# A linear-attention and gated-FFN kernel: one small transpose moved from TensorE to VectorE, finer weight loads, zero matmuls in later banks, separate places for the last outputs, and a new instruction order

## The chip, the cores and the metric

The kernel runs on one core of a Trainium2 chip. The metric is the device time of one execution in microseconds (us). A kernel is run several times; medians are quoted. Profiles are of one execution each, so a profile's span differs by a fraction of a per cent from the median.

Names used below: TensorE is "PE" in the profile (its weight loads are "PEld"), VectorE is "DVE", ScalarE is "ACT", GpSimd is "POOL" and SyncE is "SP". "SPq", "ACTq" and "POOLq" are DMA issues on an engine's queue. The kernel's matmuls write into eight accumulators of 128 x 512 fp32 in PSUM, called banks here. To "evict" a bank is to copy its result out of PSUM.

## The reference

```python
# q, k, v: [8 batches, 8 heads, 576 rows, 64]; w_phi: [64, 128]
def phi(x):
    proj = x @ w_phi
    proj = proj - max(abs(proj), axis=-1)
    return concat([exp(proj), exp(-proj)], axis=-1)

q_p, k_p = phi(q), phi(k)
kv  = k_p^T @ v                       # per batch and head
num = q_p @ kv
den = q_p . sum(k_p over rows) + 1e-6
x   = (num / den), heads side by side # [4608, 512]
out = (relu(x @ w_gate) * (x @ w_val)) @ w_out   # 512 -> 1536 -> 512
```

The subtraction of the row's maximum does not cancel: it scales the first half of the features by exp(-m) and the second half by exp(+m) after the sign is worked in. The kernel therefore takes plain exponentials and applies, for every row of q, a scale exp(2m). To get it, m has to be brought from "one row of a tile for each maximum" to "one partition for each row of q". This small turn is what the change is about.

## The kernel before

All operations are listed once in a plan, and a fixed table (`ORDER`) says in which order each engine issues them and which ring slot or bank each takes. An entry like `196P0` is operation 196 on TensorE with slot 0; `w21` is 21 zero matmuls that keep TensorE active while it has nothing to do. The kernel before has these at the start only, always in the last bank:

```python
    def warm():
        nc.tensor.matmul(warm_bank[:, 0:P], lhsT=zero, rhs=zero)
...
ORDER = """
0G 3D 9S 4D 1S 8S 11S 10S 5G 7S 6D w21 34P00 15S0 35D w3 32P1 2D 13S w1 56P230000 33A ...
"""      # over a hundred such lines
```

q's scale, done 11 times (7 times for the main rows, 4 times for the rest rows of 64): TensorE turns the maxima (`away`), VectorE reduces over the 4 groups (`amax`) and expands the result (`spread`), and a TensorE matmul in fp32 with a picking matrix brings it back (`back`).

```python
    def q_scale(mq, zq, cq, n, deps, key):
        ps = bank()
        cols = NQ * n
        one, pick = (one_a, pick_a) if n > H else (one_b, pick_b)

        def away():
            nc.tensor.matmul(ps.t[0:cols, 0:P], lhsT=mq.t..., rhs=ident32, is_transpose=True)

        def amax():
            nc.vector.tensor_reduce(ps.t[0:cols, 2 * P : 2 * P + 32], ps.t[0:cols, 0:P]..., op=ALU.max)

        def spread():
            nc.vector.tensor_tensor(zq.t[0:cols], ps.t[0:cols, None, 2 * P : 2 * P + 32]...,
                                    one[0:cols]..., op=ALU.mult)

        def back():
            nc.tensor.matmul(ps.t[:, P : P + n], lhsT=zq.t[0:cols]..., rhs=pick[0:cols])

        def ex():
            nc.scalar.activation(cq.t, ps.t[:, P : P + n], AF.Exp, scale=2.0)
        ...
```

The FFN weights come in three equal pieces of 512 columns, loaded by GpSimd's queue:

```python
    NS = 3
    def load_wide(t, w, i, key, deps=()):
        cols = slice(DFF // NS * i, DFF // NS * (i + 1))
        ...nc.gpsimd.dma_start(out=t[:, :, cols], in_=w.rearrange("(c p) n -> p c n", p=P)[:, :, cols])
```

The end of each FFN group: four blocks of 12 matmuls into a bank, an eviction by ScalarE or VectorE into one of two buffers, and a store. The last group holds the rest rows and stores each block in two parts:

```python
        "ob": ring("ob", 2, [P, DM], FP32),
        ...
        for t in range(4):
            ps, ob = bank(), buf("ob")
            ...                                   # 12 matmuls of 512 columns
            def cp(eng, ps=ps, ob=ob):
                f = nc.scalar.copy if eng is nc.scalar else eng.tensor_copy
                f(ob.t, ps.t)

            def store(t=t, ob=ob):
                if g < B:
                    ... one store on SyncE's queue
                else:
                    for x in range(2):
                        r0 = S * (2 * t + x) + SF
                        nc.sync.dma_start(out=out[r0 : r0 + SM, :], in_=ob.t[SM * x : SM * (x + 1), :])
```

## Time and profile before

| | kernel before |
|---|---|
| median of the first 3 runs | 389.31 us (389.22 to 390.38) |
| median of the 4 runs beside the changed kernel | 389.85 us (389.22 to 390.73) |
| span of the profiled execution | 388.1 us |
| TensorE's last matmul ends at | 382.40 us |
| first FFN matmul / first one of 256 columns | 34.77 / 40.61 us |

The profile page of the kernel before, first its busy time per engine, then TensorE's busy tenths and granted clock in 40 slices of the span, then its three FFN groups ("busy, mean ns of one | idle before, what ended it"):

```profile
PE 371.2 (96%) x3302; PEld 209.6 (54%) x3348; DVE 268.7 (69%) x673; ACT 234.0 (60%) x525; POOL 167.4 (43%) x199
PE   7788999999999999999999999999999999999994
PEclk9998999999999999999999999999999999999999
L714 PE MATMUL ps<-wo_sb,h 128*128 128x512 bf16 x418 | 102.2, 379 | 0.9 <-issue 0.2
L684 PE MATMUL ps<-xT,wg_sb 128*128 128x512 bf16 (+2 forms) x467 | 98.0, 336 | 0.8
L684 PE MATMUL ps<-xT,wv_sb 128*128 128x512 bf16 (+2 forms) x464 | 96.5, 338 | 1.2 <-ACT xT L663 0.2
```

TensorE bounds the kernel, and most of its time is FFN. What is not at its limit is the first four slices (about 39 us) and the last one. The windows view of the kernel before gives the columns: stretch and its length, busy time and count on PE, PEld, DVE, ACT and POOL, granted clock, DMA share, GB/s:

```profile
30.00:35.00 5.00, 3.58 (x54) 2.59 (x53) 4.83 (x16) 4.98 (x11) 3.39 (x5) 0.97 1.22 286
34.00:36.00 2.00, 1.44 (x16) 1.24 (x16) 2.00 (x9) 1.97 (x6) 1.10 (x2) 0.68 0.91 147
36.00:38.00 2.00, 2.00 (x22) 2.00 (x20) 1.78 (x5) 1.79 (x6) 1.37 (x2) 0.50 1.28 206
350.00:370.00 20.00, 19.89 (x93) 9.06 (x93) 5.97 (x10) 4.98 (x9) 0.00 (x0) 1.00 0.07 27
```

Two things are to be seen. From 30 to 35 us TensorE has work for 3.58 of 5 us while VectorE and ScalarE are full; they are the limit there. And from 34.74 to 38.15 us, by the clock record of the trace, TensorE runs at half the clock. In the FFN alone (350 to 370 us), 93 matmuls of 512 columns take 20 us, 215 ns each.

The groups by form of the kernel before that belong to q's scale (7 of its 11 times; the matmul and its weight load appear twice each because an fp32 matmul is issued as two):

```profile
L554 PEld LDWEIGHTS ps<-pick_a,zq 128*128 128x128 f32 x14 | 2.5, 190 | 0.7
L554 PE MATMUL ps<-pick_a,zq 128*128 128x32 f32 x14 | 2.3, 244 | 0.0
L546 DVE TENSOR_TENSOR zq<-ps,one_a 128x128 f32<-128x128 f32 x7 | 2.0, 290 | 0.2
```

One of those fp32 pairs in the timeline of the kernel before, between its neighbours. The pair starts at 63.72 and the next matmuls at 64.04 us: 0.32 us of TensorE for 8 columns.

```profile
63.40 0.40 PE L656 MATMUL ps<-ident,xu 128*128 128x128 bf16 x4
63.72 0.38 PE L554 MATMUL ps<-pick_b,zq 32*128 32x8 f32 x2
64.04 0.42 PE L615 MATMUL ps<-kv,qp 128*128 128x65 bf16 x8
```

The tail of the kernel before, from the timeline. In brackets is the time that an engine was idle, and what it waited for:

```profile
380.73 1.67 PE L714 MATMUL ps<-wo_sb,h 128*128 128x512 bf16 x7
380.93 4.18 SPq L733 DMA_DIRECT2D out_dram<-ob  x5
382.03 0.58 ACT L724 COPY ob<-ps 128x512 f32<-128x512 f32 x1 [3.28 <-DMA out_dram<-ob]
383.39 0.58 ACT L724 COPY ob<-ps 128x512 f32<-128x512 f32 x1 [0.78 <-DMA out_dram<-ob]
```

The last eviction starts at 383.39 us, 1.0 us after the last matmul's end, because it waits for the store that still holds its buffer.

To split the 382.4 us, I costed every TensorE instruction of the order with intervals read from the trace (0.2155 us for 512 columns, 0.109 for 256, 0.055 for 128, 0.031 for 65, and so on) and added them up. This estimate gives about 351 us of work, so about 31.5 us are lost. Comparing the running sum with the clock time at q's first scale transpose (52.59 us, 28.9 us of work done) shows where: 23.7 us before it, about 8 after it.

### The profile page before, as it was taken

Reading aid. Unit: us, or ns where it says so; the run is one execution under the profiler, and the core shown is the slowest. Engines: PE = TensorE matmul, PEld = TensorE weight load, DVE = VectorE, ACT = ScalarE, POOL = GpSimd, SP = SyncE. Lnnn points to the kernel's source line nnn. Section 1 sums busy time; section 2 is a strip of 40 time slices with the busy share of each in tenths; the row PEclk is TensorE's granted clock in tenths of the full one; section 3 lists DMA queues with packets and bytes.
Section 4 is the critical chain, followed back from the end, with each engine's and each line's share of the span. In section 5 each row is a group of like instructions: output and inputs, shape, how many; then the busy total and the mean of one; then the engine's idle time right before and its main releaser. Section 6 shows DMA issues by size and latency. Waiting matters only on the chain.

```text
span 388.1 us, 8687 instructions
## 1 busy us (share of the span) xinstructions
PE 371.2 (96%) x3302; PEld 209.6 (54%) x3348; DVE 268.7 (69%) x673; ACT 234.0 (60%) x525; POOL 167.4 (43%) x199
## 2 busy tenths in 40 slices
PE   7788999999999999999999999999999999999994
PEld 6666798644654455446546454555365444444441
DVE  5899889568787878877876898678867544514130
ACT  3999984389629956694796468953975212212211
POOL 3587935229536932693286246813831300100000
PEclk9998999999999999999999999999999999999999
DMA  7999993879877955685699765277511100200024
GB/s 194 166 136 239 142 173 44 123 146 212 124 118 201 227 130 117 78 114 107 119 207 209 135 98 131 73 171 123 95 57 15 32 10 27 69 27 27 2 108 109
DMA packets 84393, 45.00 MB, mean 116 GB/s; under 512 B 56608, under 2 KB 77728, under 8 KB 84352
## 3 DMA queue, kind: packets, MB, share of 16 engines
q0 software_dynamic: 31744, 21.83, 34.9%
q1 hardware_dynamic: 52528, 22.59, 25.6%
q8 instruction: 26, 0.43, 0.5%
q14 instruction: 15, 0.12, 0.1%
q10 hardware_dynamic: 80, 0.03, 0.0%
HBM read 37.81 MB, written 9.44 MB: 122 GB/s over the span
## 4 chain that ended last, share of the span: by engine, by line
PE 60%; DMA 3%; POOL 3%; issue 2%; DVE 1%; SPq 1%; ACT 0%; POOLq 0%; ACTq 0%
PE ps L684 34%; PE ps L714 16%; PE ps L615 4%; PE ps L482 3%; POOL vs L415 2%; DMA vn<-in_v_dram 2%; PE ps L506 1%; PE ps L389 1%; DMA xT<-xu 1%; DMA out_dram<-ob 1%; PE ps L554 0%; SPq L733 0%; DVE mq L516 0%; ACT ob L724 0%; POOL vs L422 0%
## 5 line engine op out<-in xcount | busy, mean ns | idle before, releaser
L690 ACT CAST val<-ps 128x512 bf16<-128x512 f32 (+2 forms) x132 | 66.1, 522 | 100.0 <-PE ps L684 95.7
L693 DVE SCALAR_TENSOR_TENSOR h<-ps,val 128x512 bf16<-128x512 f32 (+2 forms) x132 | 74.6, 582 | 45.9 <-PE ps L684 40.1
L714 PE MATMUL ps<-wo_sb,h 128*128 128x512 bf16 x418 | 102.2, 379 | 0.9 <-issue 0.2
L684 PE MATMUL ps<-xT,wg_sb 128*128 128x512 bf16 (+2 forms) x467 | 98.0, 336 | 0.8
L684 PE MATMUL ps<-xT,wv_sb 128*128 128x512 bf16 (+2 forms) x464 | 96.5, 338 | 1.2 <-ACT xT L663 0.2
L643 POOL TENSOR_TENSOR xu<-u,r 128x512 bf16<-128x512 f32 x36 | 37.4, 1043 | 118.8 <-DVE r L640 77.2
L354 ACT ACTIVATE qp<-ps 128x512 bf16<-128x512 f32 x144 | 81.4, 630 | 6.4 <-PE ps L506 4.1
L354 ACT ACTIVATE kp<-ps 128x512 bf16<-128x512 f32 x128 | 70.6, 618 | 7.4 <-PE ps L389 5.8
L684 PEld LDWEIGHTS <-wv_sb 128*128 128x128 bf16 x528 | 46.6, 99 | 40.0 <-issue 1.6
L684 PEld LDWEIGHTS <-wg_sb 128*128 128x128 bf16 x528 | 46.2, 98 | 40.5 <-issue 2.1
L415 POOL TENSOR_TENSOR vs<-vn,ek 128x1024 bf16<-128x1024 f32 x31 | 59.1, 1908 | 13.9 <-PE ps L615 5.0
L714 PEld LDWEIGHTS <-h 128*128 128x128 bf16 x432 | 40.2, 98 | 45.6 <-issue 2.1
L400 DVE TENSOR_REDUCE mk<-ps 128x4 f32<-128x512 f32 x64 | 42.1, 675 | 5.2 <-PE ps L389 3.4
L516 DVE TRANSPOSE_TENSOR_REDUCE mq<-ps 128x16 f32<-128x512 f32 x56 | 37.4, 695 | 4.8 <-PE ps L506 2.4
L630 DVE TENSOR_TENSOR u<-ps,t 128x195 f32<-128x195 f32 (+3 forms) x120 | 37.3, 328 | 1.7
L615 PEld LDWEIGHTS <-qp 128*128 128x128 bf16 x640 | 29.7, 98 | 14.1 <-issue 2.0
L623 DVE TENSOR_TENSOR t<-ps,cq 128x195 f32<-128x195 f32 (+1 forms) x84 | 26.0, 328 | 15.9 <-PE ps L615 9.8
L615 PE MATMUL ps<-kv,qp 128*128 128x65 bf16 x640 | 33.3, 193 | 1.0 <-DVE u L630 0.5
L724 DVE COPY ob<-ps 128x512 f32<-128x512 f32 x20 | 13.6, 680 | 17.5 <-PE ps L714 15.7
L482 PEld LDWEIGHTS <-kp 128*128 128x128 bf16 x512 | 21.9, 98 | 4.8 <-issue 1.8
L482 PE MATMUL ps<-vs,kp 128*128 128x65 bf16 x512 | 23.2, 193 | 0.7 <-POOL vs L422 0.4
L724 ACT COPY ob<-ps 128x512 f32<-128x512 f32 x16 | 9.7, 604 | 18.4 <-PE ps L714 14.2
(100 smaller groups left out, 328.6 us busy)
## 6 DMA issues: line engine op xcount, KB each, us to landing
out_dram<-ob SPq DMA_DIRECT2D x32, 256.0 KB, 2.5
vn<-in_v_dram POOLq DMA_DIRECT2D x7, 1024.0 KB, 7.4
kn<-in_k_dram POOLq DMA_DIRECT2D x7, 512.0 KB, 7.2
qn<-in_q_dram POOLq DMA_DIRECT2D x7, 512.0 KB, 6.5
wg_sb<-in_moe_w_gate_dram POOLq DMA_DIRECT2D x3, 512.0 KB, 8.9
wv_sb<-in_moe_w_val_dram POOLq DMA_DIRECT2D x3, 512.0 KB, 9.5
wo_sb<-in_moe_w_out_dram POOLq DMA_DIRECT2D x1, 1536.0 KB, 13.2
wo_sb<-in_k_dram SPq DMA_DIRECT2D x4, 256.0 KB, 3.9
```

The source lines that it names most:

```text
L354: nc.scalar.activation(dst(s), ps.t.rearrange("p (c f) -> p c f", f=f), AF.Exp, scale=sign)
L400: nc.vector.tensor_reduce(m.t.rearrange("p (i x) -> p x i", x=2)[:, x], ps.t.rearrange("p (c f) -> p c f", f=F), axis=AX.X, op=ALU.max, ap ...
L415: eng.tensor_tensor(vs.t[:, :, :, 0:D], vn.t[:, 2 * u : 2 * u + 2].rearrange("p h c d -> p (h c) d")[:, :, None, :] .to_broadcast([P, 2 * ...
L482: nc.tensor.matmul(acc[:, hh, s, :], lhsT=lhsT, rhs=rhs, start=(n == 0), stop=(n == 19))
L516: nc.vector.tensor_reduce(mdst(x), ps.t.rearrange("p (h j t) -> p h j t", j=NQ, t=32), axis=AX.X, op=ALU.max, apply_absolute_value=True, a ...
L615: nc.tensor.matmul(ps.t[:, E * (2 * i + s): E * (2 * i + s + 1)], lhsT=qp.t[:, s, h, :], rhs=kv_of[b][h // 2][0].t[:, h % 2, s, :],)
L630: nc.vector.tensor_tensor(u.t[rows, lo : lo + n], ab[:, :, 0], t.t[rows, 0:n], op=ALU.add)
L643: eng.tensor_tensor(xu.t, u.t[:, :, 0:D], r.t.to_broadcast([P, H, D]), op=ALU.mult)
L684: nc.tensor.matmul(ps.t[:, 0:n], lhsT=w[:, dc, P * fi : P * fi + P], rhs=xt()[:, dc, lo:hi], start=(dc == 0), stop=(dc == NDC - 1),)
L690: nc.scalar.copy(val.t[:, 0:n], pv.t[:, 0:n])
L693: nc.vector.scalar_tensor_tensor(h.t[:, fi, lo:hi], pg.t[:, 0:n], 0.0, val.t[:, 0:n], op0=ALU.max, op1=ALU.mult,)
L714: nc.tensor.matmul(ps.t, lhsT=h.t[:, fi, P * t : P * t + P], rhs=wo_sb[:, fi, :], start=(fi == 0), stop=(fi == NFC - 1),)
```

## The change

The intent has five parts: take q's way back off TensorE, have the first FFN weights earlier by loading two smaller pieces first, let TensorE multiply zeros into a bank just ahead of that bank's use wherever it would otherwise pause, give the last group's blocks separate places, and anneal the order of all operations anew.

```diff
 def q_scale(mq, cq, n, deps, key):
-        def spread():   # VectorE, 128x128 expansion by one_a / one_b
-        def back():     # TensorE
-            nc.tensor.matmul(ps.t[:, P : P + n], lhsT=zq.t[0:cols]..., rhs=pick[0:cols])
+        def back():     # VectorE
+            nc.vector.transpose(ps.t[:, P + 32 : P + 64], ps.t[:, P : P + 32])

-    NS = 3
+    CUTS = (0, 2, 4, 8, 12)              # pieces of 256, 256, 512, 512 columns
-        cols = slice(DFF // NS * i, DFF // NS * (i + 1))
+        cols = slice(P * CUTS[i], P * CUTS[i + 1])

+            if entry[0] == "z":
+                zeros = int(entry[1:])
+                continue
...
+            order += [(self.warm(o), PE)] * zeros     # into the bank that o is about to fill

 def load_w():                                         # w_phi, both halves
-            for hh, e in enumerate((nc.sync, nc.scalar))
+            nc.scalar.dma_start(...) for hh in range(2)

 def down(eng):                                        # k's reciprocal may go to ScalarE
+            if eng is nc.scalar:
+                eng.activation(e()[:, :, 0], m_buf.t, AF.Exp, scale=-1.0)

 # end of the last group: a v tile that is free by then, four slices
+        ends = buf("vn") if g == B else None
+            for lo, hi in ((0, DM),) if g < B or t < 3 else ((0, DM // 2), (DM // 2, DM)):
...
+                    for x, e in enumerate((SP, ACT) if t == 3 else (SP, SP)):

 ORDER = """                                           # all entries written anew
-0G 3D 9S 4D 1S 8S 11S 10S 5G 7S 6D w21 ...
+0G 4D 8S 7S 9S 1S 14S0 3D 10S 5G 6S w21 ...
+... 130A z9 141P40000 29G 99P53 ...
```

The constants `one_a`, `pick_a`, `one_b` and `pick_b` and their making are gone. A padded maximum tile (`mqm`) is cleared once so that the 32x32 blocks hold defined values.

## The prediction

> **What bounds the kernel now.** TensorE: the page has it busy 371.2 of 388.1 us, 297 of them in the three FFN groups. From 350 to 370 us, FFN alone, the windows view counts 93 512-column matmuls, 215 ns each. The Trainium skill ("TensorE: Matmul & The Clock Gate", warm issue gap N/2.4 + 2.5 ns) gives 216, so this trace agrees and nothing is to be won there. Costing every matmul of the program order with intervals read from the trace gives 351 us (an estimate); TensorE ends at 382.4. So 31.5 us are lost: 23.7 before 52 us, about 7 in small pieces from 52 to 300. Behind TensorE's end come 5.7 us of tail.
>
> **The start.** ScalarE and VectorE are the limit (mostly 4.6 to 5.0 us busy in each 5 us from 15 to 35, windows view) and TensorE starves. The first FFN matmul is at 34.8 us. From about then to 38.1 us the granted clock is 0.5, after microseconds of gaps in TensorE; that costs about 1.7 us.
>
> **What the change does.**
> 1. q's scale: the fp32 pair that turned it back leaves TensorE (11 times; the next matmul starts 0.15 to 0.32 us later: -2.7 us). VectorE loses an expansion of 0.29 us and gains a 32x32 transpose of that or less. TensorE is the limit from 50 us on, so nearly all of it counts.
> 2. Smaller first FFN weights, sooner: in the new order the second chunk's reciprocal comes about 4 us of VectorE work earlier, so the first FFN matmul can start at about 31.5 us. ScalarE and VectorE still limit; the 256-column FFN matmuls come only about 2 us earlier.
> 3. Zeros (38 more in all) fill gaps among the early attention and should keep the clock up. Points 2 and 3 together: -2.3 us.
> 4. Tail: today the last eviction waits for the store that holds its buffer (ScalarE waits 0.78 us for the output DMA and starts 1.0 us after the last matmul). Separate places end that: -0.9 us. The halved eviction is not last in the new order (a full 512-column block with two stores on one queue is), so halving gives nothing.
> 5. The new order in the steady part: -0.8 us, uncertain; the former was tuned too, and much of the 7 us looks like the cost of switching weights.
>
> Sum about -7 us. **Predicted 382.3 us (-1.8%), range 378.8 to 385.8.** Chances: faster by over 2% 0.40, within 2% 0.58, slower 0.02.
>
> **What would show each step.** Groups: no fp32 scale matmul, 11 VectorE transposes of 0.15 to 0.3 us, FFN still 215 ns apart. Timeline: first FFN matmul at 31 to 32.5 us, first 256-column one at 38.5 to 39.5 (before: 40.6). Windows: granted clock 1.00 through 40 us. Tail: last matmul to end of span 4.6 to 5.0 us, ScalarE not waiting for the output DMA. TensorE's last matmul ends at about 376.5.
>
> **What would make it wrong.** Faster: the new order recovers much of the 7 us of small losses, or ScalarE's early work moves forward by more than 2 us. Slower: the weights land after 32 us because more loads share the queue; the clock falls elsewhere; zeros hold TensorE when data is already there; a wait for a bank or ring that the ordering did not foresee.

## More of the kernel before

The start of the kernel before, from the timeline (start, length, engine, line, operation): the first exponential of k, q's first turn, the first FFN matmul, the first of 256 columns, and the first of q's scale transposes.

```profile
7.61 0.60 ACT L354 ACTIVATE kp<-ps 128x512 bf16<-128x512 f32 x1
...
14.68 0.62 PE L325 MATMUL ps<-ident,qn 128*128 128x128 bf16 x8 [1.07 <-DMA qn<-in_q_dram]
...
34.77 0.63 PE L684 MATMUL ps<-xT,wv_sb 128*128 128x128 bf16 x4
...
40.61 0.60 PE L684 MATMUL ps<-xT,wv_sb 128*128 128x256 bf16 x4
...
52.59 0.31 PE L533 MATMUL ps<-ident,mq 128*128 128x128 f32 x1
```

## The result

| | before | changed |
|---|---|---|
| median, same rounds, 4 runs each | 389.85 us (389.22 to 390.73) | 383.93 us (383.57 to 384.8) |
| ratio | | 0.985, 95% interval 0.982 to 0.9879 |
| span of the profiled execution | 388.1 us | 381.6 us |
| TensorE's last matmul ends at | 382.40 us | 376.47 us |
| mean granted clock | 0.993 | 0.999 |
| first FFN matmul / first of 256 columns | 34.77 / 40.61 us | 30.52 / 37.63 us |

Ratios here and below are the mean time of one kernel's runs over the mean of the other's runs of the same rounds, so they are not quite the ratios of the medians. The change made the kernel 1.5% faster, which is inside the band of 2%.

The page of the changed kernel, the same three lines as above:

```profile
PE 367.8 (96%) x3330; PEld 207.1 (54%) x3376; DVE 263.4 (69%) x650; ACT 238.2 (62%) x546; POOL 169.0 (44%) x201
PE   7898999999999999999999999999999999999994
PEclk9999999999999999999999999999999999999999
```

The windows view of the changed kernel, the same stretches and columns:

```profile
30.00:35.00 5.00, 4.50 (x82) 3.93 (x80) 4.89 (x20) 4.48 (x14) 2.32 (x4) 1.00 1.12 304
34.00:36.00 2.00, 1.79 (x29) 1.46 (x28) 1.97 (x8) 2.00 (x6) 1.80 (x2) 1.00 1.40 198
36.00:38.00 2.00, 2.00 (x29) 1.37 (x26) 2.00 (x7) 2.00 (x6) 0.27 (x1) 1.00 1.57 192
350.00:370.00 20.00, 19.89 (x100) 9.85 (x101) 6.19 (x10) 4.96 (x10) 0.00 (x0) 1.00 0.07 27
```

From 30 to 35 us TensorE has 4.50 us of work in place of 3.58, and the half clock is gone. The last row holds some matmuls of 256 columns, hence the higher count; TensorE is as full as before.

The groups by form of q's scale in the changed kernel:

```profile
L543 DVE STREAM_TRANSPOSE ps<-ps 128x32 f32<-128x32 f32 x11 | 2.5, 228 | 0.2
L546 ACT ACTIVATE cq<-ps 128x32 f32<-128x32 f32 x7 | 1.8, 259 | 2.2 <-DVE ps L543 2.2
```

Eleven transposes of 228 ns stand in place of the expansion (290 ns) and the fp32 pair. The Trainium skill ("VectorE: DVE Perf Modes", "The three transpose paths") says that VectorE turns a grid of independent 32x32 blocks and not a whole 128x128 tile. That is enough here, because after the maximum over the four groups only 32 columns are left, and the reference was met.

The start of the changed kernel, from the timeline:

```profile
7.22 2.89 ACT L350 ACTIVATE kp<-ps 128x512 bf16<-128x512 f32 x5
...
12.78 0.61 PE L321 MATMUL ps<-ident,qn 128*128 128x128 bf16 x8
...
30.52 0.38 PE L669 MATMUL ps<-xT,wv_sb 128*128 128x128 bf16 x4
...
37.63 0.60 PE L669 MATMUL ps<-xT,wv_sb 128*128 128x256 bf16 x4
...
50.58 0.28 PE L531 MATMUL ps<-ident,mq 128*128 128x128 f32 x1
```

q's first turn no longer waits for q. The first scale transpose comes 2.0 us earlier, and by the running sum TensorE has done 30.27 us of work by then in place of 28.9. So the loss up to this point fell from 23.7 to 20.3 us, by 3.4.

The tail of the changed kernel:

```profile
375.02 1.46 PE L707 MATMUL ps<-wo_sb,h 128*128 128x512 bf16 x6
375.55 3.22 SPq L734 DMA_DIRECT2D out_dram<-vn  x5
376.51 0.59 ACT L718 COPY vn<-ps 128x512 f32<-128x512 f32 x1 [0.99 <-PE ps L707]
```

ScalarE now starts the last eviction right behind the last matmul (376.51 after 376.47). But five stores stand in a row on SyncE's queue, 3.22 us for the five, and three of them are issued after the last matmul, the last one 1.7 us after it. From TensorE's end to the end of the span it was 5.70 us before, and is 5.13 now.

### The profile page after: what moved, and what is told of

Its sections match the earlier page's. It is cut to its first block, busy times and chain, and to the rows that moved or that the text cites. A ratio compares the mean times of both kernels' runs of the same rounds, so it can differ in the third digit from the quotient of the medians.

```text
span 381.6 us, 8751 instructions
## 1 busy us (share of the span) xinstructions
PE 367.8 (96%) x3330; PEld 207.1 (54%) x3376; DVE 263.4 (69%) x650; ACT 238.2 (62%) x546; POOL 169.0 (44%) x201
## 5 line engine op out<-in xcount | busy, mean ns | idle before, releaser
L675 ACT CAST val<-ps 128x512 bf16<-128x512 f32 (+2 forms) x132 | 67.3, 530 | 73.8 <-PE ps L669 68.9
L678 DVE SCALAR_TENSOR_TENSOR h<-ps,val 128x512 bf16<-128x512 f32 (+2 forms) x132 | 75.5, 585 | 53.3 <-PE ps L669 38.9
L707 PE MATMUL ps<-wo_sb,h 128*128 128x512 bf16 (+1 forms) x427 | 102.0, 373 | 0.7 <-issue 0.2
L669 PEld LDWEIGHTS <-wv_sb 128*128 128x128 bf16 x528 | 45.8, 98 | 40.7 <-issue 1.8
L707 PEld LDWEIGHTS <-h 128*128 128x128 bf16 x444 | 41.3, 98 | 43.4 <-issue 1.8
L600 PEld LDWEIGHTS <-qp 128*128 128x128 bf16 x640 | 30.9, 98 | 16.0 <-issue 1.2
L600 PE MATMUL ps<-kv,qp 128*128 128x65 bf16 x640 | 35.1, 193 | 0.5 <-ACT kp L350 0.2
L718 ACT COPY ob<-ps 128x512 f32<-128x512 f32 x20 | 11.6, 597 | 25.8 <-PE ps L707 24.0
L482 PE MATMUL ps<-vsm,kpm 128*128 128x65 bf16 x128 | 20.6, 193 | 0.0
```

Of the source, the lines that this page charges most:

```text
L482: nc.tensor.matmul(acc[:, hh, s, :], lhsT=lhsT, rhs=rhs, start=(n == 0), stop=(n == 19))
L600: nc.tensor.matmul(ps.t[:, E * (2 * i + s): E * (2 * i + s + 1)], lhsT=qp.t[:, s, h, :], rhs=kv_of[b][h // 2][0].t[:, h % 2, s, :],)
L669: nc.tensor.matmul(ps.t[:, 0:n], lhsT=w[:, dc, P * fi : P * fi + P], rhs=xt()[:, dc, lo:hi], start=(dc == 0), stop=(dc == NDC - 1),)
L675: nc.scalar.copy(val.t[:, 0:n], pv.t[:, 0:n])
L678: nc.vector.scalar_tensor_tensor(h.t[:, fi, lo:hi], pg.t[:, 0:n], 0.0, val.t[:, 0:n], op0=ALU.max, op1=ALU.mult,)
L707: nc.tensor.matmul(ps.t[:, lo:hi], lhsT=h.t[:, fi, P * t : P * t + P], rhs=wo_sb[:, fi, lo:hi], start=(fi == 0), stop=(fi == NFC - 1),)
```

## The experiments

The open question is which part of the change earned what. The prediction's account is pairs -2.7, start (weights and clock) -2.3, tail -0.9, steady part -0.8. The rivals are that the clock alone earned the start, that the smaller pieces did, that the new order did, or that the order gained in the steady part. Twelve runs were made in three groups, two of them of the changed kernel unaltered. All gave a correct result. The names that begin with b_ are the kernel before with a part of the change added, in its former order; those that begin with a_ are the changed kernel with a part altered.

One measure is used throughout. The first exponential of k on ScalarE moved between 6.2 and 8.7 us from one run to another, with the landing of k's first loads. From that exponential to q's first scale transpose, though, the changed kernel took 43.35 to 43.40 us in seven executions (its own, those of the two controls and of four kernels altered elsewhere) whose starts ranged from 7.22 to 8.41 us. I call this stretch "the early stretch"; in the changed kernel it takes out the scatter of the first loads. In the former order it does not do so fully: there it also holds TensorE's wait for q's first load, which was 1.07 us in the kernel before, 1.03 in b_tail, 1.93 in b_transpose, 2.25 in b_all3 and 3.50 in b_zeros.

| kernel | median, us | ratio to before, 95% interval | TensorE ends, us | early stretch, us |
|---|---|---|---|---|
| before (profiled with the changed kernel) | 389.85 | | 382.40 | 44.98 |
| changed | 383.93 | 0.985 (0.982 to 0.9879) | 376.47 | 43.36 |
| b_transpose | 387.94 | 0.9936 (0.9913 to 0.9959) | 380.43 | 45.07 |
| b_tail | 389.22 | 0.9958 (0.9939 to 0.9978) | 384.16 | 45.47 |
| b_zeros | 390.51 | 0.9992 (0.9971 to 1.0013) | 383.33 | 46.24 |
| b_all3 | 387.35 | 0.9901 (0.9881 to 0.9921) | 380.68 | 44.86 |
| a_same | 385.32 | 0.9868 (0.983 to 0.9905) | 377.48 | 43.35 |
| a_noz | 384.57 | 0.9847 (0.9813 to 0.988) | 377.75 | 43.95 |
| a_whole | 385.17 | 0.9862 (0.9831 to 0.9894) | 377.74 | 43.36 |
| a_tail2 | 384.69 | 0.9856 (0.9821 to 0.989) | 380.29 | 43.40 |
| a_ctl2 | 384.64 | 0.9826 (0.9789 to 0.9862) | 377.76 | 43.36 |
| a_back3 | 391.54 | 1.0004 (0.9971 to 1.0037) | 384.14 | 43.35 |
| b_all4 | 388.56 | 0.9911 (0.9869 to 0.9953) | 381.97 | 46.90 |
| a_tail3 | 385.64 | 0.9847 (0.9809 to 0.9886) | 377.12 | 43.36 |

The median of the kernel before was 390.69 us beside the four b_ kernels from b_transpose to b_all3, 390.31 beside a_same to a_tail2, and 391.5 beside the last four.

### b_transpose: the way back alone, in the former order

```diff
-        def spread(): ...tensor_tensor(zq...)          # VectorE
-        def back():   ...matmul(..., rhs=pick)         # TensorE
+        def spread():
+            nc.vector.transpose(ps.t[:, P + 32 : P + 64], ps.t[:, P : P + 32])
+        def back():
+            pass
```

> The kernel before, its order untouched, with the way back of q's scale alone taken from TensorE to VectorE's 32x32 transpose (the mqm tile padded with zeros, as the change does). Theory (TensorE is the limit from 50 us on, so its work counts one for one; the 11 fp32 pairs delay the next matmul by 0.15 to 0.32 us each): 2.3 to 2.9 us less than before, nearly all after 50 us of the span. Rival (the pair hides in waits or weight loads, the gain of the whole change comes from the order): under 1 us less.

It gained 0.64% of 390.69 us, 2.5 us, give or take 0.9. The trace allows another reading: from q's first scale transpose to the last of the eleven there are ten ways back. The last transpose of the kernel before, then the first and the last of b_transpose:

```profile
300.58 0.27 PE L533 MATMUL ps<-ident,mqm 128*32 128x128 f32 x1
...
52.94 0.30 PE L532 MATMUL ps<-ident,mq 128*128 128x128 f32 x1
...
299.04 0.27 PE L532 MATMUL ps<-ident,mqm 128*128 128x128 f32 x1
```

The stretch took 246.10 us in place of 247.99. That is 1.9 us over ten, or 0.19 us for one pair. But this rests on one profile of each, and the other profiles show the scatter: 248.19 and 248.84 us in b_tail and b_zeros, which keep the pairs, 247.02 and 247.50 in b_all3 and b_all4, which do not. The means of the two sorts differ by 1.5 us, or 0.15 us for one pair. The early stretch (45.07 against 44.98 us) hardly changed.

### a_back3: 33 fp32 pairs put back on TensorE

```diff
         def away(): ...
+            for i in range(3):
+                nc.tensor.matmul(ps.t[:, 2*P + 32*i : 2*P + 32*(i+1)], lhsT=ident32, rhs=ident32[:, 0:32])
```

> The changed kernel with three dummy fp32 pairs of the removed shape (128x128 weights, 32 columns) after each of the 11 first transposes of q's scale, results unused: three times the removed TensorE work. Theory (each pair takes 0.19 us of a TensorE that is the limit, as 1.9 us over 10 pairs between 52 and 300 us in the kernel with the transpose alone say): 5.5 to 8 us slower than the control. Rival (TensorE has room there, the gain of the transpose came from its shorter chain to the exponential): under 3 us slower.

The changed kernel lost all that it had gained. The groups by form of a_back3 show the 33 pairs as 66 weight loads and 66 matmuls:

```profile
L536 PEld LDWEIGHTS ps<-ident 128*128 128x128 f32 x66 | 8.4, 194 | 0.3
L536 PE MATMUL ps<-ident 128*128 128x32 f32 x66 | 8.3, 262 | 0.0
```

Against a_ctl2, which is the unaltered kernel in the same rounds, TensorE's end moved from 377.76 to 384.14 us and the median by 6.9 us: 0.19 to 0.21 us for each of 33 pairs. From the first to the last scale transpose, thirty of the pairs, a_back3 took 257.89 us, where seven profiles of kernels with the changed kernel's order there took 250.88 to 253.46: 0.15 to 0.23 us for each. Eleven pairs are thus worth 2.1 to 2.3 us, with 1.6 to 2.6 not excluded, probably a little less than the prediction's 2.7. The extra pairs also delay the maximum that follows them, so this run alone does not part TensorE's work from a longer chain to the exponential. The view of waits does: between 53 and 300 us TensorE waited for other engines for only 0.8 us in the kernel before and 0.6 us in a_back3, and never for the exponential of q's scale. It is the work that counts. The busy times in the two lines, 8.3 and 8.4 us, overstate the cost, since the load and the matmul overlap each other and their neighbours.

### b_tail: separate places for the last group, in the former order

```diff
+                place = lambda t=t: R["vn"].tiles[0].rearrange("p h c d -> p (h c d)")[
+                    :, DM * t : DM * (t + 1)]
-                f(ob.t, ps.t)
+                f(place(), ps.t)
```

> The kernel before with only the last group's output rows given four separate places, so that no eviction waits for a store. Theory: the last eviction starts 0.1 us after the last matmul instead of 1.0 us; from the last matmul to the end of the span about 4.8 us instead of 5.7; total 0.6 to 0.9 us less. Rival (the stores follow one another on one queue anyway): under 0.3 us less.

From TensorE's end to the end of the span it was 4.84 us in place of 5.70, so 0.86 us gained, just as predicted for the changed kernel. The ratio, 0.42% or 1.6 us, has an interval that reaches down to 0.9 us and so agrees with the trace at its edge. What is left of the tail is mostly the last store, issued 1.21 us after the last matmul and landed 2.38 us later.

This run also priced the clock, unasked. In its profile the half clock lasted 6.83 us, from 32.87 to 39.70, twice as long as in the kernel before:

```profile
33.00:39.60 6.60, 5.82 (x63) 4.92 (x61) 5.85 (x20) 5.95 (x16) 4.57 (x5) 0.50 1.24 223
```

TensorE waited as long for q (1.03 against 1.07 us) and the order of the early part is the same, and the early stretch was 45.47 us in place of 44.98: 0.5 us for 3.41 us more of half clock, in one pair of profiles.

### b_zeros: 29 zero matmuls ahead of eight bank uses between 27 and 35 us, in the former order

```diff
+    plan.warm = lambda o=None: Op(PE, 0.11, lambda: warm(o.banks[0].t if o else warm_bank), ...)
...
-... 196P0 ... 151P50 ... 166P21220 ... 198P5 ...
+... z6 196P0 ... z3 151P50 ... z3 166P21220 ... z4 198P5 ...     # and four more places
```

> The kernel before with only 29 zero matmuls put ahead of eight bank uses between 27 and 35 us. Theory (the half clock from 34.8 to 38.1 us comes from too little TensorE activity in the microseconds before it): the granted clock stays 1.00 from 30 to 40 us and the total is 1.0 to 1.7 us less. Rival (the fall has another cause, or the start is held by ScalarE and VectorE so the clock costs nothing): the clock falls all the same, or it stays up and the total changes by under 0.5 us.

The windows view of b_zeros shows that the zeros did what they are for:

```profile
34.00:36.00 2.00, 1.66 (x32) 1.46 (x32) 1.87 (x8) 1.73 (x5) 1.27 (x2) 1.00 1.35 167
36.00:38.00 2.00, 1.41 (x24) 1.21 (x22) 1.85 (x8) 2.00 (x8) 1.21 (x2) 1.00 1.15 176
```

The clock stayed full where it had been half. Yet TensorE, now at full clock, was busy for only 1.41 us of the next two, and the first 256-column matmul came at 40.61 us, exactly as before. The time did not change (0.9992). In this execution the clock fell in another place, from 15.66 to 19.07 us, right after q's first turn had waited 3.5 us for q's load; so b_zeros alone does not price the clock cleanly.

### b_all3: transpose, tail and zeros together, in the former order

The edit is those of b_transpose, b_tail and b_zeros together.

> The kernel before, in its own order, with all three parts: transpose, separate places at the end, zeros. Theory: they add up, 4 to 5 us less than before, so that the new order, the smaller weight pieces and the new order of the first loads are worth the remaining 1 to 2 us of the change's 5.9. Rival (the new order is what matters): under 2.5 us less.

It gained 0.99%, 3.9 us, a little less than the 4 to 5 us expected. In the profiled execution the clock was full from 10 us to the end of the work, and the early stretch was 44.86 us: 0.12 us less than before with its half clock. That understates the clock, since TensorE waited 2.25 us for q here and 1.07 us before. Against b_transpose, which had the half clock and a wait of 1.93 us, it is 0.2 us. So three of the five parts bring between half and three quarters of the change's gain (0.99% of 1.3 to 1.7%), and little of it in the early stretch. The view of waits between 8 and 30 us still shows q's first turn held by q's load (what waits, what for, total us, times, longest):

```profile
PE ps L333 <- DMA qn<-in_q_dram: 2.3, 1, 2.3
```

### a_same and a_ctl2: the changed kernel, unaltered, as controls

There is no edit. The two stand beside the other runs of their group.

> The changed kernel itself once more, as the control for the runs of this call: 1.4 to 1.6 per cent less than before, granted clock 1.00 through 40 us in the profile, first FFN matmul at 30 to 32 us.

> The changed kernel once more, control for this call: 1.3 to 1.5 per cent less than before.

They gave 0.9868 and 0.9826, beside 0.985 for the first measurement, each just outside what was expected, on opposite sides. The scatter between groups is thus about 0.4%, and a difference between two of the altered kernels below that is read from traces, not from ratios. From q's first scale transpose to the last, they took 251.13 and 251.93 us, where the first profile of the changed kernel had 250.88 (and a_tail2, whose order is the same there, 253.46).

### a_noz: the changed kernel without its 31 z zeros

```diff
-... 130A z9 141P40000 29G ...
+... 130A 141P40000 29G ...                # and every other z entry removed
```

> The changed kernel without its 31 zeros ahead of bank uses (the 90 others stay). Theory formed from the zeros put into the kernel before (they kept the clock up there but gained only about 0.3 us, unclear): the clock may fall once between 26 and 36 us, the total changes by under 1 us. Rival (the prediction's: zeros are worth 1.7 us): 1.2 to 2 us slower than the control.

The windows view of a_noz shows the half clock back, earlier than in the kernel before:

```profile
30.00:32.00 2.00, 1.88 (x23) 1.88 (x23) 1.78 (x7) 1.30 (x4) 1.30 (x2) 0.52 1.12 370
32.00:34.00 2.00, 2.00 (x31) 1.97 (x30) 1.29 (x4) 1.86 (x6) 0.00 (x0) 0.62 1.09 289
```

The mean clock was 0.993 to 0.994 in each of its six runs, so this is no accident of one execution. What it cost can be read from the two ends of its early stretch in the timeline:

```profile
7.15 2.89 ACT L350 ACTIVATE kp<-ps 128x512 bf16<-128x512 f32 x5
...
51.10 0.28 PE L531 MATMUL ps<-ident,mq 128*128 128x128 f32 x1
```

This is 43.95 us against 43.36 with the zeros: 0.6 us, and no more. The ratio shows no loss at all (0.9847 beside 0.9868 for a_same). With b_all3 (0.2 us) and b_tail (0.5 us) a step of half clock of 3.41 us is worth between 0.2 and 0.6 us, where the prediction had put it at 1.7.

### a_whole: the first weight piece loaded whole

```diff
         cols = slice(P * CUTS[i], P * CUTS[i + 1])
+        if i == 0:
+            cols = slice(0, P * CUTS[2])         # 512 columns at once
         def go():
+            if i == 1:                            # a 32 KB load in the second piece's place
+                return nc.gpsimd.dma_start(out=scrap, in_=w_phi)
```

> The changed kernel in its own order, with the first FFN weights again in pieces of 512 columns: the first load of each matrix brings columns 0 to 511 and the second a small dummy of 32 KB, so that the number and order of operations stay. Theory (the start is held by ScalarE and VectorE, weights of 512 columns in this place of the order land soon enough): first FFN matmul within 1 us of the control's, total within 0.6 us. Rival (the small pieces are what lets the FFN start 4 us earlier): first FFN matmul at 33 us or later, total 1 to 3 us slower.

The first FFN matmul came at 31.00 us (31.30 in a_same), the early stretch was 43.36 us, the ratio 0.9862 beside 0.9868. The smaller pieces are worth nothing that these runs can show. The run leaves the loads in their new, earlier place, though: the first piece of `wv` was issued at 10.59 us (10.37 in the changed kernel) and landed at 20.89. In the kernel before it was issued at 23.71 us and landed at 33.20, too late for an FFN matmul at 30.52. So the earlier place was needed, as part of the new order; the smaller size was not.

### b_all4: b_all3 with part of the new order of the first loads

```diff
-            for hh, e in enumerate((nc.sync, nc.scalar))   # w_phi on two queues
+            nc.scalar.dma_start(...) for hh in range(2)    # both on ScalarE's
-0G 3D 9S 4D 1S 8S 11S 10S 5G 7S
+0G 3D 9S 4D 1S 8S 10S 11S 5G 7S                            # k's third quarter before its fourth
```

> The kernel before in its own order with transpose, separate places, zeros, and now also the first loads in the changed kernel's manner: both loads of w_phi on ScalarE's queue, and the third quarter of k ahead of the fourth, so that q's first load (which waits for that quarter) is issued about 1.2 us sooner. Theory (q's first load is what holds ScalarE back around 13 to 16 us; the kernels in the former order wait 1.0 to 3.5 us for it, those in the new order do not): TensorE waits under 1 us for q, the first 256-column FFN matmul comes 0.7 to 1.5 us sooner than in the run without this (40.2 us), total 0.5 to 1.2 us less than that run's 0.9901 of before. Rival (the annealed order of VectorE and ScalarE is what counts): within 0.3 us of it.

In the former order q's first load waits until the third quarter of k has landed, and that quarter was loaded last, behind w_phi. In b_all4 q's load was issued at 6.30 us, near the changed kernel's 6.29 (before: 7.77), and q's wait shrank to 0.9 us. But the gain was eaten at once. The view of waits of b_all4 between 8 and 30 us:

```profile
ACT qp L361 <- PE ps L513: 3.7, 1, 3.7
PE ps L573 <- DVE vsm L469: 2.7, 1, 2.7
DVE vsm L463 <- DMA vm<-in_v_dram: 2.2, 1, 2.2
PE ps L332 <- DMA qn<-in_q_dram: 0.9, 1, 0.9
```

Read from the bottom up: v's load of rest rows (vm) now comes late (its two loads landed at 13.46 and 16.25 us, 10.21 and 11.12 in b_all3), VectorE waits 2.2 us for it, TensorE 2.7 us for VectorE, and ScalarE 3.7 us for TensorE. In the former order one of v's loads waits for k's fourth quarter, which is now the late one, so vm's loads were issued 0.85 us later than in b_all3; and with q's load now issued before them, they took 5.85 and 7.99 us to land in place of 3.45 and 3.71. The early stretch grew to 46.90 us, and its runs spread from 385.49 to 390.3 us. So half of the new order of loads is worth nothing, or less; loads have to be reordered together with what hangs on them.

### a_tail2: the half block last, stores shared by two queues

```diff
-            for x, e in enumerate((SP, ACT) if t == 3 else (SP, SP)):
+            for x, e in enumerate((SP, SP) if t == 2 else (SP, ACT)):
 # and in the order: the last block's second half last, evicted by VectorE
-... 2067P 1983S 2055P 2068D 2070A 2048P 2056A 2049P 2076A 2057S 2069S 2050A 2058S 2051S 2052S ...
+... 2067P 1983S 2055P 2068D 2070A 2069S 2072P 2056A 2073P 2057S 2058A 2074D 2075S 2076A
```

> The changed kernel with a mended end: the half row block is now the last to be computed (256 columns, evicted by VectorE in about 0.42 us), and the last stores are shared by the queues of SyncE and ScalarE, where the changed kernel has five stores one after another on SyncE's queue, 0.64 us each. Theory (that queue is the end of the tail): from the last matmul to the end of the span 4.0 us instead of 5.1, total 0.8 to 1.3 us less than the control. Rival (landing alone sets the tail): under 0.3 us less.

From TensorE's end to the span's end it was 4.71 us in place of 5.12 in a_same, so 0.4 us gained in the tail, where 1.1 were expected. The last store was issued 0.6 us sooner after the last matmul (1.09 us), but took 2.56 us to land in place of 2.33. The ratio (0.9856 beside 0.9868) does not resolve it, and the profiled execution was a long one of its kernel (386.88 us).

### a_tail3: the last full eviction shared between ScalarE and VectorE

```diff
+                    if both:            # last block of the order
+                        nc.scalar.copy(place()[:, 0:256], ps.t[:, 0:256])
+                        return nc.vector.tensor_copy(place()[:, 256:512], ps.t[:, 256:512])
 # and stores: three on SyncE's queue, two on ScalarE's
```

> The changed kernel with its end mended another way, TensorE's order untouched: the last eviction is halved between ScalarE and VectorE, three of the last five stores stay on SyncE's queue and two go to ScalarE's, and the store of the early half block no longer stands behind the late ones. Theory (five stores in a row on one queue, 0.64 us each, put the last issue 1.6 us after the last matmul): last issue 0.5 us after it, last matmul to end of span 4.0 us instead of 5.1, total 0.8 to 1.2 us less than the control. Rival (as in the first attempt, the transfers themselves limit): 4.7 us or more, under 0.5 us less.

The tail was 4.88 us, 0.26 less than a_ctl2's 5.14, where 1.1 were expected, so the rival (the transfers limit) was nearer. VectorE's half waited for ScalarE's half (the timeline has it idle until ScalarE's write of the same tile), so the halving itself gave little, and the last store took 2.62 us to land. In ratio it was 0.9847 beside 0.9826, not resolved either. No version is shown to be faster than the changed kernel.

## Why the prediction was right

The total was right: 382.3 us was said, 383.93 us measured, inside the range, and in the band "within 2%" that was called most likely. TensorE's last matmul was said to end at about 376.5 us and ended at 376.47. Some of that closeness is luck: in the two controls it ended at 377.48 and 377.76, and the terms of the sum differ:

| term | predicted, us | measured, us | read from |
|---|---|---|---|
| 11 fp32 pairs off TensorE | -2.7 | -2.2 (-1.6 to -2.6) | a_back3, b_transpose |
| start | -2.3 | -3.0 | early stretch and running sum |
| tail | -0.9 | -0.6 | TensorE's end to the span's end |
| steady part | -0.8 | about 0 (-0.25 to +0.8) | first to last scale transpose |
| first loads landed earlier in this execution | 0 | -0.4 | first exponential, 7.61 and 7.22 us |

The measured terms add up to about -6.2 us with the steady part at zero; the two profiled spans differ by 6.5.

**Pairs.** The mechanism was right and the size probably a little high. The gap behind a pair was read at 0.15 to 0.32 us in single places; the mean over the run is about 0.2 (0.15 to 0.23).

**Start.** The size of the sum was near, the reason was mostly wrong. The prediction put 1.7 us on the half clock. Removing the dip in the former order (b_all3 against b_transpose) gave 0.2 us, doubling it (b_tail) cost 0.5 and letting it back in the new order (a_noz) 0.6. How much half clock there is differs between executions: the 33 further runs of the kernel before have mean clocks of 0.980 to 0.994, so its profile with 0.993 shows a mild case. The reason is in the prediction itself, two sentences earlier: ScalarE and VectorE limit this stretch. A TensorE at full clock finishes its pieces sooner and then waits for them, as b_zeros shows (1.41 us busy of 2 at full clock). The smaller pieces gave nothing by their size (a_whole). What remains is the new order with the engine choices that belong to it: against b_all3, which has the transposes and the zeros, the early stretch is shorter by 44.86 - 43.36 = 1.50 us and holds 30.27 - 28.9 = 1.37 us more TensorE work, 2.9 us together. Part of that is q's first load: TensorE waited 2.25 us for it in b_all3 and not at all in the changed kernel, where q had landed at 11.80 us, before the turn at 12.78. The prediction did name one way in which the order would help (the second chunk's reciprocal sooner, so the first FFN matmul near 31.5 us), and that matmul came at 30.52 and 31.30 us in two executions; the first of 256 columns, said to come at 38.5 to 39.5 us, came at 37.63. Which part of the order makes the 2.9 us is not settled: the order of first loads taken half (b_all4) did not give it, and moving the first weight loads alone, or VectorE's and ScalarE's early work alone, was not tried.

**Why the clock fell.** The prediction said "after microseconds of gaps in TensorE". As a sum this holds: in the 6.8 us before the fall TensorE's pauses add up to 2.0 us. But none was long: between 26 and 36 us the longest gap in the kernel before was 0.42 us. The Trainium skill ("TensorE: Matmul & The Clock Gate", "Part 1: The HAM clock gate") gives a clock that is either full or half and falls after an idle window of about 3.4 us; the 0.50 and the 3.41 us of this trace (6.83 us, two such windows, in b_tail) agree with the states and the length, but no window before this fall was idle. Its rule in "Why this matters for your kernels", "No PE-idle gaps >~3µs between matmul bursts", was kept here and did not protect. Its section "A second HAM failure mode: psum-queue depth-cycling" comes nearer: there many very short pauses between groups of matmuls bring the clock down.

A count over the traces says more. Their clock records change in steps of 3.41 us. For every step at full clock in the 14 profiles, over 1500 in all, the columns of the matmuls that start in it were added up, transposes and zeros included. The clock fell after the 20 steps with 3226 columns or fewer (14 of them at a kernel's end) and stayed full after all others, the lowest of which had 3344. By an estimate from the 215 ns, a step full of FFN matmuls holds about 8100. Three rivals do not sort the steps:

- Pauses and busy share: a step of b_all3 with 2.26 us of pause, busy for 0.44 of its time, kept the clock (4096 columns); the step before the fall in the kernel before had 1.08 us of pause and was busy for 0.68 (3226 columns).
- Work without transposes: that same step had 2714 columns without them and was followed by the fall; one of a_whole had 2064 and was not.

Little work in a step is what goes with the fall, and the zeros fit in, since they add columns. This pattern was found afterwards and its edge is narrow; no run was made to test it.

**Tail.** The wait for the buffer went, as said. But the prediction looked at the eviction and not at the stores behind one another on SyncE's queue, so the tail came to 5.13 us where 4.6 to 5.0 was said: the changed kernel issues three of them after the last matmul, the last one at 1.71 us, and b_tail, with a tail of 4.84, two, the last one at 1.21. With fewer stores on that queue, a_tail2 and a_tail3 came to 4.71 and 4.88. That the halved eviction is not last in the order, and gives nothing, was right.

**Steady part.** The -0.8 us was not there, as far as the running sum (an estimate) can tell. Between the first and the last scale transpose the kernel before loses 7.95 us beyond its work, 247.99 for 240.04; the changed one loses 7.70, and 7.95 and 8.75 in the two controls. That the stretch was tuned out already is a guess.

## What to carry to other kernels

Ask what a stretch is limited by before pricing a fault of another engine in it: TensorE's half clock cost at most 0.6 us here because ScalarE and VectorE set the pace, while 11 small fp32 pairs in a stretch that TensorE limits were worth about 2 us. Price a small operation by the mean over many (take ten away, put thirty back), not by the gap behind one of them. When a last wait in a tail is removed, look at once for the next queue in line, and when first loads are reordered, follow everything that is gated on each of them.

## What the runs showed of the hardware that was not expected

- The clock fell to half with no TensorE pause over 0.42 us in the ten microseconds around the fall, and the zeros, 31 small matmuls in all, kept it full.
- In the 14 profiles the clock fell after every full-clock step of 3.41 us with 3226 columns or fewer and after none with 3344 or more, transposes and zeros counted.
- From one execution to the next, with the same first loads, the first exponential moved by 2.3 us (6.43 in b_zeros, 8.68 in b_tail), and from there to about 51 us the changed kernel's order repeated to within 0.05 us in seven profiles.

## What the Trainium skill lacked or had wrong

- "TensorE: Matmul & The Clock Gate", "Why this matters for your kernels": the rule of no idle gaps over about 3 us is not enough. With gaps of 0.42 us at most the clock went to 0.50 for 3.41 us. The page's "A second HAM failure mode: psum-queue depth-cycling" has the nearer case, without a figure for how little work is too little; here the edge lay between 3226 and 3344 matmul columns in a step of 3.41 us.
- The same page, "Back-to-back issue gap": it states a sustained 131 ns for matmuls of 512 columns and 216 ns for the isolated gap. Here, in 20 us of nothing else, each with its own weight load, 93 took 215 ns each, which agrees with the second and not with the first.
- No page that I read gives what a small fp32 matmul costs a busy TensorE: about 0.2 us here (0.15 to 0.23) for the two instructions of a matmul with 128x128 weights and 32 columns.
- "VectorE: DVE Perf Modes", "The three transpose paths": no duration for a 32x32 transpose from PSUM to PSUM in fp32; 128x32 took 228 ns here.
- No page that I read gives a measured spacing, in time, of stores behind one another on SyncE's queue: 0.51 to 0.65 us from one issue to the next here, where no wait lay between.
